# Regrouping k^T v, loading W_up and W_down later, and single attention tiles in a linear-attention block with a gated FFN

## The chip, the cores and the metric

One core of a Trainium2 chip runs the whole kernel. The metric is the device time in microseconds (us) of one execution; the time given for a kernel is the median of its runs. The profile is of one further execution, and its times are counted from the start of that execution's span.

## The reference: what is computed

One pre-norm block over `x` of 2048 rows and 640 columns (bf16): a linear attention with 32 heads of 20 columns, and then a gated feed-forward network of width 1536.

```python
qkv = layernorm(x) @ wqkv                      # q, k, v: [32 heads, 2048, 20]
pq, pk = q @ w_phi, k @ w_phi                  # one 20x20 matrix for each head
phi_q = concat(softmax(pq), softmax(-pq))      # 40 features; phi_k likewise
kv = phi_k^T @ v                               # [32, 40, 20], summed over all rows
z  = sum of phi_k over all rows
o  = (phi_q @ kv) / (phi_q . z + 1e-6)
h  = x + o @ wo
h2 = h + (gelu(layernorm(h) @ w_gate) * (layernorm(h) @ w_up)) @ w_down
```

`kv` needs every row of k and v before any row of `o` can be made.

## The kernel before, in words

The rows are cut into 16 tiles of 128, and four tiles make a block (4 blocks). The order of nearly everything is written out by hand, for TensorE and for the DMA queue of SyncE (SP) above all; a tile pool decides only which buffer a tile gets.

**First part, tiles 0 to 15 (about the first 70 us).** For each tile `t` the loop runs `k_tile(t)` (k projection, L284, and two exponentials on ScalarE, L317), now and then some `kv_tile(i)`, then `v_mm(t + 4)` (v projection, also L284) and the layer norm of tile `t + 6` on ScalarE (L143). That normalised tile is turned round by a DMA transpose (L159) into `LN1T`, from which `v_mm` of that tile reads two turns later. `k_norm(t)` makes `Vt[t]` (v divided by the softmax sum) on VectorE and GpSimd (L332). `kv_tile(i)` is 40 very small matmuls (L351, each with a weight load of 32 columns) that add `phi_k^T v` of tile `i` into one PSUM tile, `kvp`. The table `KVG` says behind which `t` which tiles' `kv_tile` are issued. In turn 15, `q_mm(0)` to `q_mm(3)` follow (L373, matmuls of 512 columns; each group is one PSUM tile of up to two parts, evacuated by `q_exp` on ScalarE, L378). After the loop come `kv_tile` of tiles 12 to 15 and `kv_mask`, two VectorE operations that copy `kvp` to `KV`.

**Weights of the second part.** In turn 13 the SP queue issues the loads of `Wg` (W_gate, 1920 KB), `Wo` (800 KB) and `Wu` (W_up, 1920 KB), L510 to L512; the two halves of `Wd` (W_down, 960 KB each, L529) are issued when the buffers of the first part are free.

**Second part.** `q_mm(4)`, `attn_a(0)`, and so on: for each tile, `attn_a` multiplies phi_q by `KV` (40 small matmuls, L558, and copies to SBUF), `attn_b`, `attn_b2`, `attn_b3` divide by the denominators, `attn_c` is the `Wo` projection (L632), `attn_d` adds the residual, and the last steps make the layer norm, transposed in `LN2T`. Between these the FFN runs: `gate_up` (L692) and `down` (L711), as units that `weave` walks through; a stage `(i, fn, t)` is issued just ahead of unit `i`.

From the point `split` on, PSUM is handed out as eight single banks. A `gate_up` takes two, a `down` unit one, `attn_c` two, and `attn_a_mm` four. Tiles 8 to 15 go through `attn_pair`: the matmuls of two tiles in a row, which together take all eight banks, and then the copies of both.

```python
    weave(gus(0, 256, 512) + downs(0, (2, 3)),
          attn_at(7, 0, SHORT) + [(12, split), (14, attn_pair, 8), (16, attn_pair, 10)] + attn_rest(8, 15) + ...
```

Of the kernel before, what the change touches and what calls it, by code (L numbers as in the profile page):

```python
# [17 lines left out]
def kernel(  # L18
# [12 lines left out]
    nc = tc.nc  # L31
# [21 lines left out]
    QT = (15, 15, 15, 15)  # L53
    T3 = 3

    KVG = {5: (0, 1), 9: (2, 3, 4, 5), 13: (6, 7, 8, 9), 15: (10, 11)}
    VC = Dh + 1
    KC = Dh + 2

# [161 lines left out]
    def fold(WT, W2, quarters, ds=range(NC)):  # L221


        n, w = (2, QF) if quarters else (1, HD)
        runs = []
        for c in range(NC):
            lo, hi = H0[c] * Dh, (H0[c] + NH[c]) * Dh
            for r in range(2 * n):
                a, b = max(lo, r * w), min(hi, (r + 1) * w)
                if a < b:  # L230
                    runs.append((r // n, r, c, a, b))
        runs.sort()
        for d in ds:
            wa = gtile("wa")
            wr = wa.rearrange("p u (q x) -> p (u q) x", q=n)
            for i, (u, r, c, a, b) in enumerate(runs):
                nc.tensor.matmul(wr[:, r, a - r * w:b - r * w], lhsT=WT[:, c, d * P:(d + 1) * P],  # L237
                                 rhs=BD[:, c].rearrange("p a b -> p (a b)")[:, a - H0[c] * Dh:b - H0[c] * Dh],
                                 start=(i == 0 or runs[i - 1][0] != u),
                                 stop=(i + 1 == len(runs) or runs[i + 1][0] != u), skip_group_check=True)  # L240
            dst, src = W2[:, d, :].rearrange("p (u f) -> p u f", u=2), wr[:, :, 0:w]
            if quarters:
                dst = W2[:, d, :].rearrange("p (c r f) -> p r c f", c=NC, r=4)
                src = src.rearrange("p r (c f) -> p r c f", c=NC)
            if d in (QA if quarters else KA):
                nc.scalar.copy(dst, src)
            else:
                nc.vector.tensor_copy(dst, src)
# [95 lines left out]
    def kv_tile(t):  # L344

        for s in range(2):
            for c in range(NC):
                i, h, n = SLOT[c]
                for r in range(4):
                    f0, h0 = r * QF + c * 32, r * QH + h  # L350
                    nc.tensor.matmul(kvp[QUAD[r], s * SL + i:s * SL + i + n, :],  # L351
                                     lhsT=Ek[t][:, s, f0:f0 + 32], rhs=Vt[t][:, s, h0:h0 + n, :],
                                     start=(s == c == t == 0), stop=(t == NT - 1), skip_group_check=True)
# [10 lines left out]
    def q_mm(j, part=(0, 1)):  # L364

        if 0 in part:
            pqs[j] = gtile("pq")
        for i, bc in enumerate(QG[j]):
            if i not in part:
                continue  # L370
            b, c = divmod(bc, NC)
            for kc in range(NC):
                nc.tensor.matmul(pqs[j][:, i, :], lhsT=Wq2[:, kc, c * P:(c + 1) * P], rhs=LN1T[b][:, kc, :],  # L373
                                 start=(kc == 0), stop=(kc == NC - 1))
# [87 lines left out]
    for t in range(NT):  # L462
        if t == T3:
            ps_cm.close()
            psG = ps_cm.enter_context(tc.tile_pool(name="psG", bufs=3, space=PSUM, reuse_waits="tile"))
            psK = ps_cm.enter_context(tc.tile_pool(name="psK", bufs=1, space=PSUM, reuse_waits="tile"))
            kvp = psK.tile([P, 2 * SL, VC], F32, name="kvp")
        k_tile(t)
        if t == 0:
            ln_ap(6)  # L470
        if t in FQ:
            fold(WqT, Wq2, True, [i for i, f in enumerate(FQ) if f == t])
        for j in range(len(QT)):
            if t == QT[j]:
                q_mm(j)
                q_exp(j)
        for i in KVG.get(t, ()):
            kv_tile(i)
        if 0 < t < NT - 4:
            v_mm(t + 4)  # L480
        if t > 0 and t + 6 < NT:
            ln_ap(t + 6, on_act=True)
        if 0 < t < NT - 4:
            v_ev(t + 4)
        if t % 2 == 0 and t + 8 < NT:
            ln_st(t + 8, t + 9)
        k_norm(t)
        load_T(WqT, 0, *[i for i, f in enumerate(LQ) if f == t])
        if t == 10:
            transpose_to(LN1T[0][:, :, P:2 * P], ln_a(1), False)  # L490
        if t == 12:
            ln_ap(0, on_act=True)
        if t == 7:
            nc.gpsimd.memset(kmask[QUAD[0]], 1.0)
            for k, lo, n, base in ((3, 0, 2, 0), (2, 6, 3, 12)):
                m = kmask[QUAD[0], lo:lo + 6].rearrange("p (k n) -> p k n", k=k)
                nc.gpsimd.affine_select(out=m, in_=m, pattern=[[4, k], [-Dh, n]],
                                        compare_op=ALU.is_ge, fill=0.0, base=base, channel_multiplier=1)
                nc.gpsimd.affine_select(out=m, in_=m, pattern=[[-4, k], [Dh, n]],
                                        compare_op=ALU.is_ge, fill=0.0, base=Dh - 1 - base, channel_multiplier=-1)  # L500
        if t == 8:
            nc.gpsimd.memset(KV, 0.0)
        if t == 9:
            for r in (1, 2, 3):
                nc.sync.dma_start(kmask[QUAD[r]], kmask[QUAD[0]])
        if t == 11:
            nc.gpsimd.tensor_copy(KV[:, 0, :, KC - 1], kmask)
            nc.gpsimd.tensor_copy(KV[:, 1, :, 0], kmask)
        if t == 13:
            nc.sync.dma_start(Wg, wg_v)  # L510
            nc.sync.dma_start(Wo, wo_v)
            nc.sync.dma_start(Wu, wu_v)  # L512
    q = len(QT)
    for t in range(12, NT):
        kv_tile(t)
# [9 lines left out]
    p2r = ctx.enter_context(tc.tile_pool(name="p2r", bufs=1, side="right", reuse_waits="tile"))  # L525
    Wd = p2r.tile([P, NF, D], BF16, name="Wd")
    wd_v = B_w_down.rearrange("(c p) n -> p c n", p=P)
    for f in (0, NF // 2):
        nc.sync.dma_start(Wd[:, f:f + NF // 2], wd_v[:, f:f + NF // 2])  # L529

    ABs = [p2r.tile([P, 2, H, KC], F32, name=f"AB{i}") for i in range(2)]
    ABs += [LN1F[:, i * 2 * H * KC:(i + 1) * 2 * H * KC].rearrange("p (s h f) -> p s h f", s=2, h=H) for i in range(2)]
# [10 lines left out]
    def attn_a_mm(t):  # L543

        b = t // 4
        if b not in LN2T:
            LN2T[b] = p2.tile([P, NC, 512], BF16, name="LN2T", bufs=2)
        if psB:
            ab = [bank("ab") for r in range(4)]
        else:  # L550
            st[t, "ab"] = gtile("ab"), gtile("ab")
            ab = [x[:, i] for x in st[t, "ab"] for i in range(2)]
        for s in range(2):
            for c in range(NC):
                i, h, n = SLOT[c]
                h += s * QH
                for r, q in enumerate(QUAD):
                    nc.tensor.matmul(ab[r][:, h * KC:(h + n) * KC], lhsT=eq(t, c, s)[q],  # L558
                                     rhs=KV[q, s, i:i + n].rearrange("p h f -> p (h f)"),
                                     start=(s == c == 0), stop=(s == 1 and c == NC - 1), skip_group_check=True)  # L560
        st[t] = ab

    def attn_pair(t):

        for i in (t, t + 1):
            attn_a_mm(i)
        for i in (t, t + 1):
            AB = ABs[i % len(ABs)]
            for r in range(4):
                (nc.scalar.copy, nc.vector.tensor_copy)[r % 2](  # L570
                    AB[:, :, r * QH:(r + 1) * QH].rearrange("p s h f -> p s (h f)"),
                    st[i][r][:, 0:2 * QH * KC].rearrange("p (s x) -> p s x", s=2))
            st[i] = AB

    def attn_a(t, dve=0):
        attn_a_mm(t)
        AB, ab = ABs[t % 2], st[t, "ab"]
        for u in ((1, 0) if t in (4,) else (0, 1)):
            (nc.vector.tensor_copy if u >= 2 - dve else nc.scalar.copy)(
                AB[:, :, u * UH:(u + 1) * UH].rearrange("p s (r h) f -> p r s (h f)", r=2),  # L580
                ab[u][:, :, 0:2 * QH * KC].rearrange("p r (s x) -> p r s x", s=2))
        st[t] = AB

# [166 lines left out]
        return [(down, b, tl, u) for tl in tls for u in range(2)]  # L750


    q_mm(q)
    attn_a(0, 1)
    q_exp(q)
    q_mm(q + 1)
    attn_b(0, True)
    attn_b2(0, True)
# [48 lines left out]
    def attn_rest(t, i):  # L807
        return [(i + o, fn, t) for fn, o in zip((attn_b, attn_b2, attn_b3, attn_c, attn_d, attn_d2, attn_e), LONG)]
# [4 lines left out]
          attn_at(2, 0, (-1, 0, 1, 2, 7, 7, 8, 10)) + attn_at(3, 1, (2, 3, 4, 5, 9, 9, 10, 12)) + attn_at(4, 6, SHORT2) + attn_at(5, 9, SHORT2) +  # L813
          attn_at(6, 13, SHORT2))
    weave(gus(0, 256, 512) + downs(0, (2, 3)),
          attn_at(7, 0, SHORT) + [(12, split), (14, attn_pair, 8), (16, attn_pair, 10)] + attn_rest(8, 15) +
          attn_rest(9, 17) + attn_rest(10, 19) + attn_rest(11, 21))
    weave(gus(1, 0, 512) + downs(1, range(4)),
          [(18, attn_pair, 12), (20, attn_pair, 14)] + attn_rest(12, 19) + attn_rest(13, 21) + attn_rest(14, 23) +
          attn_rest(15, 25))  # L820
    for b in (2, 3):
        weave(gus(b, 0, 512) + downs(b, range(4)), [])
# [31 lines left out]
```

## Time and profile before

| | before |
|---|---|
| median of 3 runs | 282.86 us (282.02 to 283.41) |
| profiled execution, its time | 283.22 us |
| profiled execution, its span | 281.2 us |
| TensorE matmul (PE) busy | 270.1 us, 96% |
| weight load (PEld) busy | 172.7 us, 61% |
| VectorE (DVE) busy | 173.7 us, 62% |
| ScalarE (ACT) busy | 140.4 us, 50% |
| GpSimd (POOL) busy | 96.4 us, 34% |
| mean granted TensorE clock | 0.987 |
| DMA | 21.46 MB, 42401 packets |
| instruction packets, queue q8 | 23, 0.38 MB |

How to read it: the span is the profiled execution from first to last instruction; its own time is 2.0 us longer, and 0.36 us above the median. PE is TensorE executing matmuls, PEld its weight loads, which run beside them. In the chain of waits, the program is followed back from its last instruction, at each step to what released it; "issue" is time in which an engine waited for nothing that the profile shows. PEclk is the TensorE clock granted by the throttle.

### The profile page before, as it was taken

To read this page: it belongs to the slowest core of one execution; us is meant where nothing else is said; L and a number is where in the kernel's file an instruction comes from. 1 tells how busy PE (TensorE), PEld (TensorE's weight loads), DVE (VectorE), ACT (ScalarE), POOL (GpSimd) and SP (SyncE) were. 2 spreads that over 40 slices of the span, in tenths; PEclk is the share of its full clock that TensorE was granted. 3 is DMA by queue.
4 is the path that set the end of the run, shared out by engine and by line. 5 is a ranking of instruction groups with operands and counts; after the bars stand their busy time and mean duration, and the time that the engine had idled before them with its cause. 6 is when DMAs were issued, how large, how long until landed. Compare 5 with 4: busy or idle time off the path is not lost.

```text
span 281.2 us, 7231 instructions
## 1 busy us (share of the span) xinstructions
PE 270.1 (96%) x2981; PEld 172.7 (61%) x2995; DVE 173.7 (62%) x332; ACT 140.4 (50%) x241; POOL 96.4 (34%) x218
## 2 busy tenths in 40 slices
PE   7999999998499999999999999999999999999996
PEld 3777777765145688778864555576455567444574
DVE  5899999995068586666558785327776432233232
ACT  5789897887069975545534245404234520222200
POOL 4248898764001123736411383201255210000000
PEclk9999999999689999999999999999999999999999
DMA  7972627699900011324220322210113411000011
GB/s 200 193 244 47 73 57 112 72 233 392 357 7 2 2 24 26 72 50 94 43 55 2 70 48 47 49 48 28 47 23 72 48 47 49 23 0 0 2 47 47
DMA packets 42401, 21.46 MB, mean 76 GB/s; under 512 B 35201, under 2 KB 40577, under 8 KB 42369
## 3 DMA queue, kind: packets, MB, share of 16 engines
q1 hardware_dynamic: 41712, 20.98, 30.9%
q8 instruction: 23, 0.38, 0.6%
q10 hardware_dynamic: 656, 0.03, 0.2%
q14 instruction: 10, 0.07, 0.1%
HBM read 10.18 MB, written 2.62 MB: 46 GB/s over the span
## 4 chain that ended last, share of the span: by engine, by line
PE 87%; DVE 4%; DMA 3%; issue 3%; ACT 2%; SPq 0%; POOL 0%; POOLq 0%
PE gu L692 37%; PE pd L711 19%; PE pq L373 8%; PE po L632 8%; PE pk L284 5%; PE pv L284 4%; PE kvp L351 2%; PE ab L558 2%; DMA Wv<-in_A_wqkv_dram 2%; DMA LN1T<-ln 1%; DVE stats L113 1%; PE wa L237 1%; DVE y L714 1%; ACT vS L304 1%; ACT E L317 1%
## 5 line engine op out<-in xcount | busy, mean ns | idle before, releaser
L695 ACT ACTIVATE g<-gu 128x512 bf16<-128x512 f32 (+1 forms) x60 | 30.7, 512 | 67.7 <-PE gu L692 66.9
L698 DVE TENSOR_TENSOR GT<-gu,g 128x512 bf16<-128x512 f32 (+1 forms) x60 | 34.4, 580 | 48.2 <-PE gu L692 39.3
L692 PE MATMUL gu<-LN2T,Wg 128*128 128x512 bf16 (+1 forms) x291 | 61.3, 335 | 0.5
L692 PE MATMUL gu<-LN2T,Wu 128*128 128x512 bf16 (+1 forms) x300 | 61.8, 336 | 0.0
L711 PE MATMUL pd<-Wd,GT 128*128 128x320 bf16 (+2 forms) x396 | 53.5, 295 | 0.0
L711 PEld LDWEIGHTS <-GT 128*128 128x128 bf16 x396 | 37.9, 98 | 14.6 <-DVE GT L698 0.2
L692 PEld LDWEIGHTS <-Wu 128*128 128x128 bf16 x300 | 29.3, 98 | 22.6
L692 PEld LDWEIGHTS <-Wg 128*128 128x128 bf16 x300 | 28.8, 98 | 21.2
L284 PEld LDWEIGHTS <-LN1T 128*128 128x128 bf16 x290 | 27.8, 98 | 10.7 <-DMA LN1T<-ln 0.2
L714 DVE TENSOR_TENSOR y<-pd,x_sb 128x320 bf16<-128x320 f32 (+2 forms) x29 | 13.9, 480 | 29.0 <-PE pd L711 29.0
L332 POOL TENSOR_TENSOR vt<-vS,rs 128x672 bf16<-128x672 bf16 x22 | 29.2, 1349 | 7.5 <-DVE rs L328 5.2
L373 PE MATMUL pq<-LN1T,Wq 128*128 128x512 bf16 x95 | 24.8, 404 | 5.2 <-issue 5.0
L632 PE MATMUL po<-Wo,oT 128*128 128x320 bf16 x160 | 24.3, 299 | 0.0
L284 PE MATMUL pk<-Wk,LN1T 128*128 128x320 bf16 x160 | 24.2, 299 | 0.0
L324 DVE TENSOR_REDUCE sk<-E 128x64 f32<-128x1280 bf16 x16 | 22.9, 1433 | 0.3 <-ACT E L317 0.3
L378 ACT ACTIVATE Eq<-pq 128x1024 bf16<-128x1024 f32 (+1 forms) x26 | 20.0, 829 | 1.8 <-PE pq L373 1.7
L632 PEld LDWEIGHTS <-oT 128*128 128x128 bf16 x160 | 15.6, 98 | 7.4 <-ACT oT L157 0.5
L284 PE MATMUL pv<-Wv,LN1T 128*128 128x320 bf16 x130 | 19.8, 299 | 0.1
L317 ACT ACTIVATE E<-pk 128x640 bf16<-128x640 f32 x28 | 18.2, 706 | 3.1 <-PE pk L284 3.0
L373 PEld LDWEIGHTS <-Wq 128*128 128x128 bf16 x100 | 9.9, 102 | 16.1 <-issue 7.2
L143 ACT ACTIVATE ln<-x_sb,v,rstd 128x640 bf16<-128x640 bf16 x14 | 12.9, 920 | 11.3 <-POOL v L671 10.8
L609 DVE TENSOR_TENSOR tt<-AB,w 128x1280 bf16<-128x1280 f32 x12 | 17.8, 1485 | 1.0 <-POOL w L602 0.9
(113 smaller groups left out, 287.5 us busy)
## 6 DMA issues: line engine op xcount, KB each, us to landing
out_dram<-y SPq DMA_DIRECT2D x15, 160.0 KB, 1.8
Wg<-in_B_w_gate_dram SPq DMA_DIRECT2D x1, 1920.0 KB, 9.3
Wu<-in_B_w_up_dram SPq DMA_DIRECT2D x1, 1920.0 KB, 14.8
Wd<-in_B_w_down_dram SPq DMA_DIRECT2D x2, 960.0 KB, 7.9
x_sb<-in_A_x_dram SPq DMA_DIRECT2D x2, 640.0 KB, 6.7
Wo<-in_A_wo_dram SPq DMA_DIRECT2D x1, 800.0 KB, 10.5
x_sb<-in_A_x_dram SPq DMA_DIRECT2D x4, 160.0 KB, 4.2
Wv<-in_A_wqkv_dram SPq DMA_DIRECT2D x2, 320.0 KB, 5.0
```

The costliest lines, as they stand in the source:

```text
L284: nc.tensor.matmul(ps[:, u, 0:HD], lhsT=lnT(t, c), rhs=W[:, c, u * HD:(u + 1) * HD], start=(c == 0), stop=(c == NC - 1))
L317: nc.scalar.activation(Ek[t][:, s, :].rearrange("p (u f) -> p u f", u=2), pk[:, :, 0:HD], ACTF.Exp, scale=((lnp[t][2], nrstd[t]) if t in C ...
L324: nc.vector.reduce_sum(sk, Ek[t].rearrange("p s (h f) -> p (s h) f", f=Dh), axis=AX.X)
L332: eng.tensor_tensor(vt[:, s], vS[t % 8], rs[:, s * H:(s + 1) * H, None].to_broadcast([P, H, VC]), ALU.mult)
L373: nc.tensor.matmul(pqs[j][:, i, :], lhsT=Wq2[:, kc, c * P:(c + 1) * P], rhs=LN1T[b][:, kc, :], start=(kc == 0), stop=(kc == NC - 1))
L378: nc.scalar.activation(Eq[j][:, :, s, :], pqs[j][:, 0:len(QG[j])], ACTF.Exp, scale=(1.0, -1.0)[s])
L609: nc.vector.tensor_tensor(tt.rearrange("p s (h f) -> p s h f", f=Dh), num, w[:, :, :, None].to_broadcast([P, 2, H, Dh]), ALU.mult)
L632: nc.tensor.matmul(pos[u], lhsT=st[t][:, c, :], rhs=Wo[:, c, u * HD:(u + 1) * HD], start=(c == 0), stop=(c == NC - 1))
L692: nc.tensor.matmul(gu[i][:, 0:n], lhsT=W[:, c, f * P:(f + 1) * P], rhs=LN2T[b][:, c, a0:a1], start=(c == 0), stop=(c == NC - 1))
L695: nc.scalar.activation(g[:, 0:n], gu[0][:, 0:n], ACTF.Gelu_apprx_tanh)
L698: nc.vector.tensor_tensor(st[b, "g", f][:, a0:a1], gu[1][:, 0:n], g[:, 0:n], ALU.mult)
L711: nc.tensor.matmul(ps, lhsT=st[b, "g", f][:, tl * P:(tl + 1) * P], rhs=Wd[:, f, f0:f1], start=(f == 0), stop=(f == NF - 1))
```

## The change

It does four things.

1. `KVG` and the order in turn 15. Before, `kv_tile` ran for 2, 4, 4 and 2 tiles in turns 5, 9, 13 and 15, and for 4 tiles behind the loop; in turn 15 the two tiles came behind `q_mm(0)` to `q_mm(3)`, so that six tiles ran in a row. Now it runs for three tiles each in turns 6, 9, 12 and 15, ahead of the q groups in turn 15, and for four tiles behind the loop.
2. The order of the weight loads. In turn 13 only `Wo` and then `Wg` are issued. `Wu` and `Wd` are issued by the new function `load_late`. It makes GpSimd copy one column of `Eq[4]` (which `q_exp(4)` writes) into `Wu`, so that the load of `Wu`, and the loads of `Wd` behind it on the SP queue, start only after `q_exp(4)`.
3. `attn_a(0)` is issued between the two parts of `q_mm(4)` (five matmuls each), not behind both.
4. `attn_pair` becomes `attn_one`, for tiles 8 to 15 one at a time, two units apart.

```diff
-    KVG = {5: (0, 1), 9: (2, 3, 4, 5), 13: (6, 7, 8, 9), 15: (10, 11)}
+    KVG = {6: (0, 1, 2), 9: (3, 4, 5), 12: (6, 7, 8), 15: (9, 10, 11)}
...
+        for i in KVG.get(t, ()):
+            kv_tile(i)
         for j in range(len(QT)):
             if t == QT[j]:
                 q_mm(j)
                 q_exp(j)
-        for i in KVG.get(t, ()):
-            kv_tile(i)
...
         if t == 13:
+            nc.sync.dma_start(Wo, wo_v)
             nc.sync.dma_start(Wg, wg_v)
-            nc.sync.dma_start(Wo, wo_v)
-            nc.sync.dma_start(Wu, wu_v)
...
-    for f in (0, NF // 2):
-        nc.sync.dma_start(Wd[:, f:f + NF // 2], wd_v[:, f:f + NF // 2])
+
+    def load_late(j):
+
+        nc.gpsimd.tensor_copy(Wu[:, 0, 0:1], Eq[j][:, 0, 1, 0:1])
+        nc.sync.dma_start(Wu, wu_v)
+        for f in (0, NF // 2):
+            nc.sync.dma_start(Wd[:, f:f + NF // 2], wd_v[:, f:f + NF // 2])
...
-    def attn_pair(t):
-
-        for i in (t, t + 1):
-            attn_a_mm(i)
-        for i in (t, t + 1):
-            AB = ABs[i % len(ABs)]
-            for r in range(4):
-                (nc.scalar.copy, nc.vector.tensor_copy)[r % 2](
-                    AB[:, :, r * QH:(r + 1) * QH].rearrange("p s h f -> p s (h f)"),
-                    st[i][r][:, 0:2 * QH * KC].rearrange("p (s x) -> p s x", s=2))
-            st[i] = AB
+    def attn_one(t):
+
+        attn_a_mm(t)
+        AB = ABs[t % len(ABs)]
+        for r in range(4):
+            (nc.scalar.copy, nc.vector.tensor_copy)[r % 2](
+                AB[:, :, r * QH:(r + 1) * QH].rearrange("p s h f -> p s (h f)"),
+                st[t][r][:, 0:2 * QH * KC].rearrange("p (s x) -> p s x", s=2))
+        st[t] = AB
...
-    q_mm(q)
+    q_mm(q, (0,))
     attn_a(0, 1)
+    q_mm(q, (1,))
     q_exp(q)
+    load_late(q)
     q_mm(q + 1)
...
-          attn_at(7, 0, SHORT) + [(12, split), (14, attn_pair, 8), (16, attn_pair, 10)] + attn_rest(8, 15) +
+          attn_at(7, 0, SHORT) + [(12, split), (14, attn_one, 8), (16, attn_one, 9), (18, attn_one, 10), (20, attn_one, 11)] + attn_rest(8, 15) +
...
-          [(18, attn_pair, 12), (20, attn_pair, 14)] + attn_rest(12, 19) + attn_rest(13, 21) + attn_rest(14, 23) +
+          [(18, attn_one, 12), (20, attn_one, 13), (22, attn_one, 14), (24, attn_one, 15)] + attn_rest(12, 19) + attn_rest(13, 21) + attn_rest(14, 23) +
```

## The prediction, made before the changed kernel was run

> **What bounds the kernel now.** The page first: PE is busy 270.1 of 281.2 us, so what PE does not wait for costs nothing. The chain of waits says the same and shows one foreign lump.
>
> ```profile
> PEclk9999999999689999999999999999999999999999
> DMA  7972627699900011324220322210113411000011
> ...
> PE 87%; DVE 4%; DMA 3%; issue 3%; ACT 2%; SPq 0%; POOL 0%; POOLq 0%
> ```
>
> The PE timeline from 55 to 125 us, in it the end of the first part (start, duration, operation; in brackets the idle time ahead of it and its releaser):
>
> ```profile
> 67.36 2.14 PE L351 MATMUL kvp<-vt,E 128*32 128x42 bf16 x240
> 74.24 0.61 PE L373 MATMUL pq<-LN1T,Wq 128*128 128x512 bf16 x1 [4.74 <-issue]
> 75.06 3.62 PE L373 MATMUL pq<-LN1T,Wq 128*128 128x512 bf16 x8 [0.22 <-issue]
> 78.62 0.63 PE L558 MATMUL ab<-KV,Eq 32*128 32x44 bf16 x40
> ```
>
> To be seen: PE idles 4.74 us between the six-tile k^T v run and `q_mm(4)`, for no semaphore that the profile shows: `q_exp(3)` ended at 69.31, `kv_mask` at 70.49. The clock dips in the same slices, and the DMA is full there (9, 9, 9). Next, the stretches, and the DMA queues from 71.6 to 71.7 us.
>
> ```profile
> core 0: us, PE busy (x) PEld busy (x) DVE busy (x) ACT busy (x) POOL busy (x), PEclk, DMA share, GB/s
> 72.60:74.20 1.60, 0.00 (x0) 0.00 (x0) 0.00 (x0) 0.00 (x0) 0.00 (x0) 0.50 1.03 358
> 74.20:79.30 5.10, 4.84 (x50) 1.95 (x52) 0.00 (x0) 0.00 (x0) 0.00 (x0) 0.50 0.65 221
> 79.40:95.00 15.60, 15.44 (x130) 8.28 (x132) 12.33 (x27) 14.60 (x21) 1.59 (x4) 1.00 0.01 1
> ```
>
> ```profile
> q1 hardware_dynamic: 23, 0.03, 96.9%
> q8 instruction: 1, 0.02, 67.9%
> ```
>
> The page counts 23 such instruction packets, 0.38 MB, 16 KB each. Spread over PE's 2981 matmuls and 2995 weight loads that is about 64 bytes each, so I read q8 as PE's own code, 256 instructions a packet. Counted along the trace's weight loads, they follow each other 256 instructions apart. This one lasts 0.679 x 16 x 0.1 us = 1.1 us, ends near 72.75, and PE resumes at 74.23. My reading: PE holds two blocks of code, asks for the next when it takes up one, and the run of 240 matmuls (480 instructions in 2.14 us) used both up while the refill stood behind `Wu` and `Wd`. By the count the refill was asked for at about 68.0, so it took 6.2 us: 3.6 to begin, 1.1 to move, 1.5 to be used.
>
> **Part 1, the refill and the clock.** In the new order the q groups (matmuls of 0.22 us) stand ahead of the last run, which has 160 matmuls, 320 instructions. The PE program is as long as before up to `q_mm(4)`, so the block boundary still falls at the end of the run and the refill is still asked for about at its start. The run lasts 1.4 us (at 2.14/240) to 1.6 (the four-tile run at 55.1 took 1.57). What changes is the DMA: `Wo` and `Wg` are 2.7 MB; at about 400 GB/s from 59.5 us they are through by 66.5, ahead of that run (start about 69.0, by part 2). So the refill begins on idle queues. For that delay the nearest row is the packet in 56.5 to 56.6 us, at most 1.5 us after the run at 55.1 began; I take 1.0 (bounds 0.8 and 1.5). Moving it takes 1.1. The time to be used is 1.5 at most (the row, under load), 0.3 at least; I take 1.1, since the row was loaded. Refill 3.2 (2.2 to 4.1), less 1.4 of run: an idle stretch of **1.8 us** (0.75 to 2.75) in place of 4.74 and 0.22. Gain 3.15.
>
> [...]
>
> The clock was 0.50 from 72.6 to 79.3. There, ten q matmuls came 0.427 us apart instead of 0.216 (2.1 us), and the 40 of `attn_a(0)` took 0.56 for 0.40. **Gain 2.3** if the clock stays up. It fell when PE had been idle since 69.50, at most 3.1 us; idle time of 1.1 us at the start (4.63 to 6.86) did not lower it. 1.8 lies between, nearer to the harmless row: I take no dip, and price one at 1.7 us (half the low stretch here, 3.4 of 6.8 us, at half speed), up to 3.4.
>
> [...] The row shows a fall after at most 3.1 us of idleness, so the dip stays a rival.
>
> **Part 2, k^T v regrouped.** The 640 matmuls are the same. Moving two tiles out of turn 5 uncovers a transfer:
>
> ```profile
> 26.40 0.81 ACT ln L143
> 27.21 0.03 ACT vS L304
> 27.23 4.08 DMA LN1T<-ln
> 31.31 0.09 issue
> 31.40 0.72 PE pv L284 x4
> ```
>
> `v_mm(9)` waits for `LN1T` of tile 9, landed at 31.31; the 0.83 us of `kv_tile(0)` and `(1)` at 30.43 lay in that wait. Without them PE stands still from 30.34 to 31.39, and the same work comes later. From 31.4 to 69.5 PE has no gap to absorb it. **Loss 0.85** (0 if the transpose lands as fast as its siblings, 2.6 us, to 1.05). `kv_tile(9)` to `(11)` need `Vt[11]`, whose GpSimd half ends at 57.57, two us ahead; `Vt[15]` ends at 67.72, before tile 15 at about 70. Other groups stay three turns behind their `Vt`. Nothing else starves: between the runs of 240 instructions lie over 4 us of larger matmuls.
>
> **Part 3, the loads.** The copy on GpSimd takes 0.24 us (the copy of L507) and waits for `q_exp(4)`; GpSimd has nothing else before 89.18, and behind `Wu` and `Wd` the SP queue has nothing until the transposes of about 100 us. So no queue is held up. Issue at about 77.5; 3.8 MB at 400 GB/s are through by about 88. The first `gate_up` was at 96.1 and comes at about 91 now; `Wu`, first in line, lands at about 84, or at 92.3 if it took the 14.8 us that it took behind `Wg` and `Wo`. `down` follows at 108. Cost nothing; 0.3 us with the slowest landing. The refill asked for inside this load has about 10 us before its block is needed.
>
> **Part 4, attn_a(0) inside q_mm(4).** Same instructions. Its copies start 1.1 us earlier against the q matmuls, and `kv_mask` (0.9 us on DVE) now has five matmuls as cover, not ten. The idle stretch covers it; if that went to nothing, 0.3 us. Zero.
>
> **Part 5, attn_one.** The chain of waits from 139 to 149 us:
>
> ```profile
> 139.69 3.27 PE pd L711 x24
> 142.97 0.02 issue
> 142.99 0.50 DVE y L714
> 143.50 0.04 issue
> 143.54 0.45 PE ab L558 x35
> 143.98 3.38 PE pd L711 x24
> ```
>
> A pair wants all eight banks, so its last matmuls wait for the residual add of the `down` unit just ended. From the pair's first matmul to the next unit it takes 1.03 us (142.89 to 143.92), the second 1.10 (147.28 to 148.38); a single tile took 0.39 (115.20 to 115.59). So two singles are 0.25 and 0.32 cheaper; two pairs in each of two weaves: 1.1 us. A single wants four banks, in the rotation last used by work at least two units old, so no new wait should appear. Copies, `attn_b` and so on follow one unit later at the earliest, and their `LN2T` is wanted a block later. I take **1.0** (0 to 1.1).
>
> **The sum.** 3.15 + 2.3 - 0.85 + 1.0 = 5.6 us, against the profiled execution: 283.22 - 5.6 = 277.6, with the span 2.0 lower. That execution lay 0.36 over the median, so the median should be **277.3 us**. The forecast's own bounds: stall 0.75 and no loss in part 2 give 275.4; stall 2.75, no gain in part 5 and 0.2 more loss in part 2 give 279.4.
>
> **Rivals.**
>
> A. *The 4.74 us are not the loads' doing*: a refill takes 6.2 us on an idle DMA too, or the pause belongs to the change of PSUM pools. Then 6.2 - 1.4 = 4.8 us remain, with the dip: 282.86 + 0.85 - 1.0 = 282.7, no change. For it: "issue" names no cause, and it sits exactly where the pools change. Against: PE resumes 1.5 us after a code packet that came 3.6 us late. 0.12.
>
> B. *The pause shrinks, but the clock still falls.* 277.3 + 1.7 = 279.0. 0.16.
>
> C. *Slower: the block before that is late.* It is asked for at about 60.4 us, inside the load of `Wo` and `Wg`; its counterpart began at 63.77, 5.1 us late. If it came only after 69, PE would starve inside the last run, ask for the next block only then, and starve again. With pauses s1 and s2 and a dip that costs 3.4 the time is 282.86 - 4.96 - 2.3 + 0.85 - 1.0 + s1 + s2 + 3.4: slower by 0.5% (1.4 us) once s1 + s2 passes 5.4, so with s2 = 2.4 when the block is usable only after 72, 11.6 us after its call. The longest delay counted is 5.1 to begin and 2.6 more. Against it, too: that load ends by 66.5. 0.05.
>
> **How the numbers follow.** Forecast 0.67, B 0.16, A 0.12, C 0.05. The measurement of this kernel tells about 0.5%, 1.4 us, from no change. The forecast and B are faster by more than that: 0.83; A is the same: 0.12; C slower: 0.05. A range of 275.4 to 280.6 holds the forecast and nearly all of B with a stall at its upper bound; A and C, 0.17, stay out.
>
> **What would show it.** Right: the gap ahead of the first `pq` behind the last k^T v run is near 1.8 us, with a code packet inside it and q1 idle; PEclk is 1.00 through it; a gap of about 1 us opens before `pv` at 31.4; the `y` to `ab` pieces are gone near 139 and 186. Wrong: a gap over 4 us there with the DMA idle (A), a clock of 0.50 after it (B), a gap inside the run (C), or `gu` waiting for `Wu`.

## The result, and the profile after

The changed kernel takes **279.85 us** (median of 6 runs, 277.84 to 280.84) against 282.72 before (6 runs): a ratio of 0.9884, with a 95% interval of 0.984 to 0.9928. It is faster, and inside the predicted range, but by 2.9 us where 5.6 were forecast. Its profiled execution, the slowest of the six, took 280.84 us with a span of 278.9.

The page of after, the clock, the DMA and the chain of waits:

```profile
PEclk9999999999889999999999999999999999999999
DMA  6963616587049112224211222110213311000011
...
PE 72%; issue 1%; ACT 0%; DVE 0%
```

The PE timeline of after, the same stretches as before the change:

```profile
31.44 1.53 PE L284 MATMUL pv<-Wv,LN1T 128*128 128x320 bf16 x10 [0.74 <-DMA LN1T<-ln]
...
61.58 7.73 PE L373 MATMUL pq<-LN1T,Wq 128*128 128x512 bf16 x34
69.23 1.47 PE L351 MATMUL kvp<-vt,E 128*32 128x42 bf16 x160
73.25 1.25 PE L373 MATMUL pq<-LN1T,Wq 128*128 128x512 bf16 x4 [2.55 <-issue]
```

The pause ahead of `q_mm(4)` shrank from 4.74 to 2.55 us; it did not go. The DMA is idle in it (a 0 among the slices, between the two loads; 7 GB/s from 70.7 to 73.2 us), so the loads are not what is moving while PE waits. The stretches of after show the clock still falling behind it, for a shorter time; the DMA queue from 70.8 to 70.9 us holds a code packet and nothing else:

```profile
70.70:73.20 2.50, 0.01 (x1) 0.00 (x0) 0.87 (x2) 0.48 (x1) 0.00 (x0) 1.00 0.02 7
73.30:74.70 1.40, 1.35 (x41) 0.62 (x43) 0.00 (x0) 0.00 (x0) 0.00 (x0) 1.00 0.05 12
74.80:78.10 3.30, 3.08 (x22) 1.20 (x10) 2.77 (x7) 1.63 (x2) 0.00 (x0) 0.50 0.00 0
```

```profile
q8 instruction: 1, 0.02, 58.3%
```

And in the FFN the waits of the pairs are gone (the chain of waits of after, 137 to 147 us; `pd` is the output of a `down` unit, `ab` that of `attn_a_mm`, and the `y` pieces of before have no counterpart):

```profile
137.88 3.26 PE pd L713 x24
141.14 0.40 PE ab L562 x39
141.53 3.37 PE pd L713 x24
144.90 0.40 PE ab L562 x39
```

The difference of the two profiled spans, 2.3 us, can be split at marks on PE (start of the first matmul of turn 5's `k_tile`, of the last of k^T v, of the first of `q_mm(4)`, of the first of `gate_up`, and the end of the last matmul):

| from ... to | before | after | difference |
|---|---|---|---|
| start to turn 5 | 28.98 | 29.18 | +0.20 |
| turn 5 to the end of k^T v | 40.34 | 41.34 | +1.00 |
| end of k^T v to `q_mm(4)` | 4.92 | 2.74 | -2.18 |
| `q_mm(4)` to `gate_up` | 21.88 | 21.04 | -0.84 |
| `gate_up` to the last matmul | 182.47 | 181.97 | -0.50 |

### The profile page after: what moved, and what is told of

Same layout as the page of the kernel before. It is cut to its first block, busy times and chain, and to the rows that moved or that the text cites. A ratio compares the mean times of both kernels' runs of the same rounds, so it can differ in the third digit from the quotient of the medians.

```text
span 278.9 us, 7232 instructions
## 1 busy us (share of the span) xinstructions
PE 270.4 (97%) x2979; PEld 172.5 (62%) x2995; DVE 173.6 (62%) x332; ACT 141.2 (51%) x241; POOL 95.8 (34%) x219
## 4 chain that ended last, share of the span: by engine, by line
PE 72%; issue 1%; ACT 0%; DVE 0%
PE gu L694 37%; PE pd L713 19%; PE po L634 8%; PE pq L373 6%; PE ab L562 2%; PE tp L156 0%; ACT Eq L378 0%; DVE y L716 0%
## 5 line engine op out<-in xcount | busy, mean ns | idle before, releaser
L700 DVE TENSOR_TENSOR GT<-gu,g 128x512 bf16<-128x512 f32 (+1 forms) x60 | 34.4, 580 | 47.3 <-PE gu L694 38.5
```

What stands on the lines that cost most here:

```text
L700: nc.vector.tensor_tensor(st[b, "g", f][:, a0:a1], gu[1][:, 0:n], g[:, 0:n], ALU.mult)
```

## The experiments

The questions: is the pause a code refill; which of the edits shortened it; what is the rest of it; and what did the other edits bring. Marks are as in the table above; "pause" is PE's idle time ahead of `q_mm(4)`. A "dip" is a stretch at a granted clock of 0.50: 72.55 to 79.38 us in the profile of before (6.83 us, mean clock 0.987), 74.74 to 78.15 in that of the changed kernel (3.41 us, 0.994). Going by these two, a run whose mean granted clock on record is 0.993 or 0.994 is counted as having one of 3.4 us, at 0.987 or 0.988 one of 6.8 us, at 0.999 or 1.0 none; the last column counts the runs that have one.

| kernel | median, us | ratio to before (95%) | pause | turn 5 to end of k^T v | `q_mm(4)` to `gate_up` | `gate_up` to end | runs with a dip |
|---|---|---|---|---|---|---|---|
| before | 282.3 to 282.7 | | 4.74 | 40.34 | 21.88 | 182.47 | 35 of 35 (6.8 us in 15, 3.4 in 20) |
| changed | 279.85 | 0.9884 (0.984 to 0.9928) | 2.55 | 41.34 | 21.04 | 181.97 | 3 of 6, and 1 of 2 more below |
| late loads alone | 279.01 | 0.9876 (0.9828 to 0.9924) | 1.97 | 40.02 | 20.94 | 182.48 | 3 of 4 |
| regrouping alone | 283.11 | 1.0011 (0.9988 to 1.0035) | 4.65 | 40.85 | 21.87 | 182.48 | 10 of 10 |
| single tiles alone | 282.17 | 0.9990 (0.997 to 1.0011) | 4.81 | 40.35 | 21.75 | 181.97 | 10 of 10 |
| changed, not regrouped | 277.36 | 0.9809 (0.9784 to 0.9835) | 2.04 | 40.79 | 19.41 | 181.97 | 0 of 5 |
| changed, W_gate late too | 277.98 | 0.9832 (0.9804 to 0.9859) | 2.01 | 41.09 | 19.41 | 181.97 | 0 of 4 |
| last six tiles interleaved | **276.44** | 0.9787 (0.9759 to 0.9814) | 0.86 | 40.55 | 19.40 | 181.97 | 0 of 4 |

**Late loads alone.** The kernel before with this edit (`load_late` is the function of the change):

```diff
-            nc.sync.dma_start(Wg, wg_v)
             nc.sync.dma_start(Wo, wo_v)
-            nc.sync.dma_start(Wu, wu_v)
+            nc.sync.dma_start(Wg, wg_v)
...
     q_exp(q)
+    load_late(q)
```

> The kernel before, with only the weight loads changed (W_o and W_gate in turn 13, W_up and W_down behind q_exp(4)); k^T v groups, attn_a(0) and pairs as before. Theory (the pause is a code refill that stood behind the loads): the refill is asked for at about 68.0 us as before and takes 4.0 us as in the changed kernel (1.6 to begin, 0.9 to move, 1.5 to be used), so PE resumes at about 72.0, a pause of 2.5 us, and no wait ahead of pv at 31.4. Time about 279.3 us (278.3 to 280.3). Rival P (the pause belongs to the change of PSUM pools, or a refill always takes 6.2 us): pause 4.7 us and a time of 282.7. Rival R (the shorter last run of k^T v made the pause shorter): pause near 4.7 us, 282.7.

Its PE timeline:

```profile
66.47 2.14 PE L351 MATMUL kvp<-vt,E 128*32 128x42 bf16 x240
70.58 3.27 PE L373 MATMUL pq<-LN1T,Wq 128*128 128x512 bf16 x9 [1.97 <-issue]
```

279.01 us and a pause of 1.97, half a microsecond under the 2.5 that the theory had, with P and R (4.7 us) out. The run is the old one of six tiles, so the shorter run is not needed for the shorter pause. This one edit gives as much as the whole change.

**Regrouping alone.** The kernel before with the new `KVG` and the new order in turn 15.

```diff
-    KVG = {5: (0, 1), 9: (2, 3, 4, 5), 13: (6, 7, 8, 9), 15: (10, 11)}
+    KVG = {6: (0, 1, 2), 9: (3, 4, 5), 12: (6, 7, 8), 15: (9, 10, 11)}
...
+        for i in KVG.get(t, ()):
+            kv_tile(i)
         for j in range(len(QT)):
...
-        for i in KVG.get(t, ()):
-            kv_tile(i)
```

> The kernel before, with only k^T v regrouped (turns 6, 9, 12, 15, ahead of the q groups); loads and pairs as before. Theory: the refill is still asked for at the start of the last run and still stands behind W_up and W_down, pause 4 to 5 us with the clock's dip, and the regrouping costs 0.85 to 1.2 us ahead of it: about 283.7 us (283 to 284.5). Rival R (the shorter run makes the pause shorter): pause 2.5 us and 281.5 us.

```profile
68.09 1.47 PE L351 MATMUL kvp<-vt,E 128*32 128x42 bf16 x160
74.22 0.61 PE L373 MATMUL pq<-LN1T,Wq 128*128 128x512 bf16 x1 [4.65 <-issue]
```

The last run takes 1.47 us and not 2.14, but it ends at 69.6 (69.5 before), and `q_mm(4)` begins at the same 74.2: rival R is out. The time is no different from before. The pieces behind that are a loss of 0.5 us between turn 5 and the end of k^T v, and 0.1 less pause.

**The code moved by 128 instructions.** The warm-up matmuls at the start are cut finer, 64 more of them with 4448 columns in all for 4608, meant to take the same time; every later PE instruction stands 128 places later.

```diff
-    warm(*[512] * 7, *[P] * 8)
+    warm(*[512] * 4)
+    for _ in range(75):
+        nc.tensor.matmul(wu[0:32, 0, 0:32], lhsT=ones[:, 0:32], rhs=ones[:, 0:32], start=True, stop=True)
```

> The kernel before, with 64 more tiny matmuls in the warm-up at the start (the warm-up takes as long as before: fewer columns each), so that every later PE instruction stands 128 places later in the code. Theory: the boundary of a 256-instruction block now falls 128 instructions ahead of the end of the six-tile run, so the pause (4 to 5 us, behind the loads) lies inside the run, between matmuls of kvp with 64 of them to go, and none is left ahead of q_mm(4). Time within 1 us of 282.7. Rival P (pool change): the pause stays ahead of the first pq matmul.

The PE timeline of this one, on the kernel before:

```profile
59.10 1.39 PE L353 MATMUL kvp<-vt,E 128*32 128x42 bf16 x144
62.10 0.29 PE L353 MATMUL kvp<-vt,E 128*32 128x63 bf16 x16 [1.61 <-issue]
...
73.03 1.61 PE L353 MATMUL kvp<-vt,E 128*32 128x42 bf16 x176
77.68 0.86 PE L353 MATMUL kvp<-vt,E 128*32 128x42 bf16 x64 [3.04 <-issue]
78.47 0.61 PE L375 MATMUL pq<-LN1T,Wq 128*128 128x512 bf16 x1
```

And from its waits (total, times, longest, in us):

```profile
PE kvp L353 <- issue: 7.1, 3, 3.0
```

The pause left `q_mm(4)` and stands inside the run, with exactly 64 matmuls to go: 128 instructions ahead of its old place, and so at the same place in the code, after 2228 weight loads and matmuls (twice the count of the weight loads that started before it). Two further pauses, without a releaser too, came up in other k^T v runs (2.48 us at 45.5 and the 1.61 above), after 1210 and 1718 by the same count, about four and two blocks of 256 earlier. In this kernel, then, the pauses belong to places in the code, not to an operation or to a change of pools. The pause took 3.04 us where 4 to 5 were expected, and the time was missed: 287.88 us (two runs, 286.46 and 289.30) for an expected 282.7. Beside the two new pauses, 1.49 us at 23.6 come from a `k_tile` that waited for `vS` on ScalarE, which is a side effect of the edit (its PSUM buffer may have been handed out differently; the trace does not show it).

> The changed kernel with the same 64 tiny matmuls in the warm-up. Theory: the block boundaries fall into the q groups and into the middle of the last four-tile run; each refill then has several us of q matmuls ahead of its need, so there is no pause at all (under 0.3 us) and no dip of the clock: 279.8 - 2.5 - 0.5 to 1.2 = about 276.5 us (275.8 to 277.3). Rival P: pause of 2.5 us ahead of the first pq, 279.8 us.

```profile
63.28 7.07 PE L375 MATMUL pq<-LN1T,Wq 128*128 128x512 bf16 x32 [0.80 <-issue]
72.27 1.24 PE L375 MATMUL pq<-LN1T,Wq 128*128 128x512 bf16 x4 [0.52 <-ACT Eq L380]
```

On the changed kernel the same edit gave 278.79 us (ratio 0.986, 0.9825 to 0.9894): no pause by code ahead of `q_mm(4)` and no dip, as expected, but 0.80 us of pause by code in the q groups (after 1974 by the count above; its code packet moved from 60.9 to 61.8 us, while `Wo` and `Wg` were still loading, and how much of its delay is theirs no run shows), 0.52 us until `q_exp(3)` had freed a PSUM buffer, and the same 1.49 us of side effect. So it is 2.3 us above the expected time, by causes that were not in it.

**The changed kernel without the regrouping.** The same lines the other way round:

```diff
-    KVG = {6: (0, 1, 2), 9: (3, 4, 5), 12: (6, 7, 8), 15: (9, 10, 11)}
+    KVG = {5: (0, 1), 9: (2, 3, 4, 5), 13: (6, 7, 8, 9), 15: (10, 11)}
```

> The changed kernel with the k^T v groups and the order in turn 15 of before (2, 4, 4, 2 tiles, then 4 behind the loop); late loads, attn_a(0) inside q_mm(4) and single tiles stay. Theory (the late loads shorten the pause, the grouping does nothing for it): pause 2.0 to 2.6 us ahead of q_mm(4) as in the loads-only kernel, no wait for LN1T of tile 9, single tiles 0.5 us cheaper from the first gate_up to the end: 278.4 us (277.6 to 279.3), not slower than the changed kernel. Rival R (the grouping is part of what shortens the pause): pause over 3.5 us, 281 us or more.

277.36 us, 2.5 us better than the changed kernel, and a pause of 2.04:

```profile
67.55 2.14 PE L351 MATMUL kvp<-vt,E 128*32 128x42 bf16 x240
71.73 1.25 PE L373 MATMUL pq<-LN1T,Wq 128*128 128x512 bf16 x5 [2.04 <-issue]
```

So the change is better with the first of its four edits taken back. By the marks its profile gains 0.55 us ahead of the end of k^T v, 0.51 in the pause, and 1.63 by a clock that does not fall. Only the first of the three is the regrouping's by its place. That the clock stays up is not shown to be its doing: late loads alone has the old grouping too, with a pause of 1.97, and its clock fell in three of four runs. Against the four runs of the changed kernel whose clock stayed up (277.84 to 279.79, median 278.3), 0.9 us are left. The time came out below the expected 277.6 to 279.3, which had allowed for a dip in some runs.

**The last six tiles between the q groups.** On top of the run above:

```diff
-    KVG = {5: (0, 1), 9: (2, 3, 4, 5), 13: (6, 7, 8, 9), 15: (10, 11)}
+    KVG = {5: (0, 1), 9: (2, 3, 4, 5), 13: (6, 7, 8, 9)}
...
                 q_exp(j)
+                for i in ((10,), (11, 12), (), ())[j]:
+                    kv_tile(i)
...
-    for t in range(12, NT):
+    for t in range(13, NT):
```

> The kernel of the run above, with the last six k^T v tiles not in one run but laid between the q groups: q0, tile 10, q1, tiles 11 and 12, q2, q3, tiles 13 to 15. The number and length of all matmuls stay. Theory: the refill wanted at q_mm(4) is asked for in tile 12, 4.5 us ahead of its need, and the one before it has 8 us; with a refill of 4.0 us on a free DMA there is no pause by code, at most 0.4 us until q_exp(3) frees its PSUM buffer, and no dip of the clock: 278.4 - 2.2 - 0.7 = about 275.7 us (275.0 to 276.7). Rival P (pool change): the pause ahead of q_mm(4) stays at 2 us or more, 278.4 us.

```profile
68.16 1.14 PE L351 MATMUL kvp<-vt,E 128*32 128x42 bf16 x120
70.16 1.24 PE L373 MATMUL pq<-LN1T,Wq 128*128 128x512 bf16 x5 [0.86 <-ACT Eq L378]
```

The wait now has a releaser: ScalarE's last `q_exp`, which held the PSUM buffer, 0.86 us for an expected 0.4. No pause by code is left, the clock stays at 1.00, and 276.44 us is the fastest kernel here: 2.1% under before, and 3.4 us under the change. So a wait for PSUM is there after all, as in rival P, but of 0.86 us; it had lain under the refill.

**Single tiles alone**, on the kernel before (and likewise for tiles 12 to 15).

```diff
-          ... + [(12, split), (14, attn_pair, 8), (16, attn_pair, 10)] + ...
+          ... + [(12, split), (14, attn_one, 8), (16, attn_one, 9), (18, attn_one, 10), (20, attn_one, 11)] + ...
```

> The kernel before, with only attn_pair replaced by attn_one. From the first gate_up to the last matmul 182.0 us in place of 182.5, as the changed kernel shows it; so 282.2 us against 282.7, not to be told from no change by the times alone. Rival (the prediction's term): 1.0 us, 281.4 to 281.8. The pause ahead of q_mm(4) stays at 4.7 us.

182.47 became 181.97 from the first `gate_up` on; the times alone cannot tell it from nothing. The rival's 1.0 us is out.

**W_gate late too**, on the changed kernel.

```diff
-            nc.sync.dma_start(Wg, wg_v)
...
-        nc.gpsimd.tensor_copy(Wu[:, 0, 0:1], Eq[j][:, 0, 1, 0:1])
+        nc.gpsimd.tensor_copy(Wg[:, 0, 0:1], Eq[j][:, 0, 1, 0:1])
+        nc.sync.dma_start(Wg, wg_v)
         nc.sync.dma_start(Wu, wu_v)
```

> The changed kernel with W_gate loaded late too, at the head of the late loads, so that from about 62 us to q_exp(4) nothing but code moves. Theory (a refill is longer while a load is on the queues): in the changed kernel the W_gate load landed at 69.5 us, in the last run; without it the refill begins 1.0 us after it is asked for and the pause is 1.9 to 2.1 us in place of 2.55, with fewer dips of the clock: 278.5 us (277.5 to 279.5). W_gate lands at about 90 us, ahead of the first gate_up at 92 to 93; if not, gate_up waits for it. Rival (the refill does not care for the load that is left): pause 2.5 us, 279.8 us.

```profile
68.36 1.47 PE L351 MATMUL kvp<-vt,E 128*32 128x42 bf16 x160
71.84 1.25 PE L373 MATMUL pq<-LN1T,Wq 128*128 128x512 bf16 x5 [2.01 <-issue]
```

Pause 2.01 us, time 277.98 (277.81 to 278.37), 1.9 us under the changed kernel and with no dip in four runs. `W_gate` landed at 86.3 and nobody waited for it. The code packet begins 1.1 us after the run did, against 1.6 in the profile of the changed kernel, where `W_gate` landed at 69.51, 0.3 us into that run. That looks like the theory, but another run speaks against it: in the kernel that was not regrouped `W_gate` landed at 69.43, just after the code packet had begun (69.35), and the pause was 2.04 all the same. So this run does not show that `W_gate` lengthens the refill.

**The changed kernel twice more**, for its spread.

> The changed kernel once more, unchanged, for a second profile. The runs of it lie between 277.8 and 280.8 us. [...]

> The changed kernel, unchanged, for a third profile. Pause 2.0 to 2.7 us; 21.0 us from q_mm(4) to the first gate_up with a dip of the clock, 19.4 us without.

```profile
72.30 1.25 PE L373 MATMUL pq<-LN1T,Wq 128*128 128x512 bf16 x5 [2.36 <-issue]
```

```profile
71.80 1.30 PE L373 MATMUL pq<-LN1T,Wq 128*128 128x512 bf16 x5 [2.17 <-issue]
```

278.35 us with a pause of 2.36, no dip, and 19.42 us from `q_mm(4)` to `gate_up`; 279.14 with a pause of 2.17, a dip, and 20.93. The shorter pause had the dip. So about 1.5 us of the spread of this kernel is the dip. That is not all of it: one of its runs took 279.79 with a mean clock of 1.0, and no trace shows why; its other cause stays open.

The third edit, `attn_a(0)` inside `q_mm(4)`, was not run alone. Late loads alone, without it, and the last profile above, with it, both had a dip of 3.4 us and took 20.94 and 20.93 us from `q_mm(4)` to `gate_up`, so nothing is to be seen of it.

## Why the prediction was right, and where its sum failed

**Right: what the pause is.** Moving the code by 128 instructions moved the pause by 128, and freeing the DMA shortened it, from 4.74 to 1.97 us with the late loads alone. Rival A is out by the pause of 2.55 us, and rival C because no gap stands inside the last run. In the trace of before a code packet began at 63.77 us, after 1718 weight loads and matmuls by the count above, and the next at 71.65; PE stopped at 69.50 after 2228, 510 instructions further on, which fits my reading of two blocks of 256. The pauses starved PE in runs of 320 and 480 instructions, for up to 4.74 us before `q_mm(4)`.

**Mis-sized: the refill, 3.2 us taken.** From the start of the last run to PE's resumption the three profiles of the changed kernel have 4.02, 3.83 and 3.65 us. The largest part is the last piece: in the six profiles with `Wu` and `Wd` out of the way (changed, twice more, loads alone, not regrouped, `W_gate` late), PE resumes 1.25 to 1.5 us after the code packet ends. I had read the 1.5 of before as swollen by load and took 1.1; with the loads out of the way it was hardly shorter. Moving the packet took 0.93, 1.29 and 1.42 us (1.1 taken). It began 1.0 to 1.2 us after the run, as taken, in the two later profiles, but 1.6 in the first. `Wg` was through later than the sum had it (landed at 69.51, not by 66.5: SP issued it at 59.2, 2.1 us later than its first weight load of before), but that is not shown to be the cause: in the kernel that was not regrouped `Wg` landed after the packet had begun, and the pause was 2.04. Why the first was late stays open. So the forecast 1.8 us of pause became 1.97 to 2.55 in the six, and 2.17 to 2.55 in the change. The gain was 2.2 to 2.6 in place of 3.15. Of the 3.15, 0.22 was no idle time: the rows of before list nine of `q_mm(4)`'s ten matmuls, and the gap of 0.22 us is where the tenth's record is missing (the profile of single tiles alone has all ten, and no such gap).

**Wrong choice: no dip of the clock (2.3 us).** Without a dip `q_mm(4)` to `gate_up` takes 19.4 us, so the dip of before cost 2.5, and the term, 2.3, was sound for the profiled run. But rival B, at 0.16, is what the profile shows: a dip that costs 1.6 (21.04 against 19.4). It came in two profiles out of three, and by the granted clock in four of the eight runs on record, so neither "no dip" nor "a dip" describes this kernel. Before, too, the profiled execution was not the only kind: it had the dip of 6.8 us, but 20 of the 35 runs of before whose clock is on record had one of 3.4 us, of which half (the clock is 0.50 in it), 1.7 us, is by my estimate the most that can be gained. The length of the pause alone does not tell which kind comes: pauses of 1.97, 2.17 and 2.55 us had the dip, pauses of 2.01, 2.04 and 2.36 had none.

**Right in place and about right in size: the regrouping's loss, 0.85.** Between turn 5 and the end of k^T v the four profiles with it as changed took 40.94 to 41.34 us, the regrouping alone 40.85; before, single tiles alone and late loads alone took 40.02 to 40.35. Against the 40.34 of before that is 0.5 to 1.0 us. (Not regrouped took 40.79, in which 0.56 us is a wait for another transpose into `LN1T`, at 47.3 us, that the other profiles do not have.) The wait for `LN1T` of tile 9 is there (0.25 to 0.74 us, by when the transpose lands), and in the first profile 0.24 us ahead of a weight fold that waited for its DMA transpose.

**Mis-sized: single tiles, 1.0.** They gave 0.50. I had compared starts of groups (1.03 and 1.10 us for a pair), and took for lost time what was not. The row to take was in the waits of before, which gives the four waits as 0.6 us in all:

```profile
PE ab L558 <- DVE y L714: 0.6, 4, 0.2
```

**Nothing, as forecast:** the late loads themselves. `Wu` landed at 88.25 in the changed kernel and `gate_up` did not wait.

The sum with measured terms: 2.2 + 0.8 + 0.5 - 1.0 - 0.2 (start) = 2.3 us, as between the two spans, 281.2 and 278.9. No error made up for another: pause, clock and single tiles all gave less than the sum had. Range and sign held because the range had room for the dip and the longer pause, and 279.85 lies in its upper part, nearer to rival B's 279.0 than to the forecast's 277.3.

## What to carry to other kernels

Many tiny matmuls in a row ran out of code here before they ran out of data (240 in 2.14 us, then 4.74 us of idle PE). The pause, without a releaser, at a fixed count of instructions and with a code packet in it, was cured by laying long matmuls between the tiny ones (no pause by code left, 0.86 us of wait for PSUM) and shortened by keeping bulk loads off that moment (4.74 us to 1.97), not by making the run a little shorter (4.65). Test each edit of a bundle by itself and by taking it away: here late loads alone brought as much as all four together, and the regrouping took 0.5 to 1.0 us back. When a pause is shortened and not removed, look for what it hid (here a PSUM buffer), and for the clock.

## What the runs showed of the hardware

- The code packets of before and after were 16 KB each (23 of them, 0.38 MB). That one holds 256 PE instructions is an estimate: 5976 weight loads and matmuls in the trace of before, over 23 packets, make 260. The pauses stood after 1210, 1718, 1974 and 2228 weight loads and matmuls, 254 or about twice that apart. On free queues a refill took 1.0 to 1.6 us to begin (counted from the start of the last run of the changed kernel, twice more and `W_gate` late), 0.9 to 1.4 to move and 1.25 to 1.5 to be used; behind the loads of before it took 3.6 to begin, if it was asked for at 68.0 as I counted. The tiny matmuls came 8.9 ns apart (240 in 2.14 us); at that pace 256 instructions, 128 of them matmuls, last 1.1 us.
- In the profiles of before and after the changes of the clock are whole multiples of 3.413 us apart: low for 6.83 and 3.41 us, high for 68.27 us ahead of that and for 201.39 behind it in both. Counted from the start of the span they came at 72.55 and 79.38 us before, at 74.74 and 78.15 after. Before, PE had been busy for 0.36 us of the 3.41 ahead of the fall (69.14 to 72.55); then for 1.50 (72.55 to 75.96) and for all of the next 3.42, and the clock was 0.50 through both. In the changed kernel PE was busy for 1.43 us of the 3.41 ahead of the fall (71.33 to 74.74), idle for 1.98, and for 3.19 of the next 3.41, at 0.50. How much idle time brings a fall is not shown: of the two later profiles of the changed kernel the one with a pause of 2.36 us kept its clock at 1.00, the one with 2.17 had the dip.
- Shifting code by 128 instructions at the very start, with 64 tiny matmuls more, cost the kernel before 5 us (two runs; 1.49 us of it is the other side effect), moved its one pause and brought two more; the same matmuls in the same order at another place in the code are not the same kernel.
